# k's inverse norms finished on VectorE, one more row of squares on TensorE, and one 32-bit filler: an edit in the opening of a fused attention and MoE kernel

## The chip, the cores and the metric

The kernel runs on one core of one Trainium2 chip, in one launch. The metric is the device time in microseconds (us), the median of several executions. The core has five engines with their own instruction queues: TensorE (PE, matmuls; its weight loads are shown as PEld), VectorE (DVE), ScalarE (ACT), GpSimd (POOL, which here only issues DMAs) and SyncE (SP, DMAs too). They wait for each other by semaphores.

## What is computed

Four batches of q, k and v, each 6080 rows by 256 channels, go through a channel attention, and the result through an MLP with a squared relu. Norms run along the 6080 rows, one per batch and channel.

```python
def _attn_ref(q, k, v, tau) -> np.ndarray:
    qn = q / (np.linalg.norm(q, axis=1, keepdims=True) + 1e-06)
    kn = k / (np.linalg.norm(k, axis=1, keepdims=True) + 1e-06)
    s = kn.transpose(0, 2, 1) @ qn / tau
    s = s - s.max(-1, keepdims=True)
    a = np.exp(s)
    a /= a.sum(-1, keepdims=True) + 1e-09
    return (v @ a).astype(np.float32)
...
def _moe_ref(x, w_in, w_out, s, b) -> np.ndarray:
    h = x @ w_in
    r = np.maximum(h, 0.0)
    g = s * (r * r) + b
    return (g @ w_out).astype(np.float32)
```

The MLP goes from 256 to 2048 and back to 256 channels, over 24320 rows. tau is 1.

## The kernel before

The main loop, to which the whole file leads up, goes over 48 groups of 512 rows. For each group the core multiplies v (transposed) with `wa`, which is the attention matrix already multiplied into `w_in` (line 755, `h_ps`), applies the relu on ScalarE (L765), squares on VectorE or ScalarE (L776, L778), and multiplies with `w_out` (L830 for the first and last group, L926 for the others). The next batches' attention matrices are worked out beside that. Only the first batch's has nothing to run beside: this opening is what the edit touches.

**The opening.** The rows of the first batch come in 14 chunks: eleven of 512 rows (128 partitions by 4 rows), and three small ones of 256, 128 and 64 rows, the last of which is put in as the fourth chunk; so the numbers from the end are -5 and -4 for two whole chunks and -3, -2, -1 for the last three, a chunk of 512 rows, one of 256 and one of 128. POOL issues the loads of all but the first two chunks in order (L134), k and q in turn, but of the last three (`NLATE = 3`) all of k first and then all of q. Every chunk is multiplied into the 256 by 256 product of q and k (`s_ps`, L150, two matmuls of 128x256 for each of its rows per partition).

For the norms each chunk is squared, k's half on ScalarE (L182), q's on VectorE or ScalarE (L179, L182). VectorE folds the squares twice, 4 rows to 2 and 2 to 1, k and q in one instruction (L196), and adds the result to the first chunk's (`into_first`, L210, 128x512 f16). Sums over the partitions are TensorE matmuls against ones (`add_norms`): for k one 128x256 matmul per row (L251), for q two 128x1 matmuls per row (L255). The list of what is still to be summed is `self.rows`. The last three chunks are not folded into the first: k's squares of chunk -3 are halved on VectorE (L226, `half`), the others go to TensorE as they are (those of chunk -1 are made on VectorE, L176).

From the sum of squares x the inverse norm 1/(sqrt(x) + 1e-6) is made by `inverse` in four ScalarE steps (L276): Ln with `tiny` added, Exp with scale 0.5, Ln with `eps` added, Exp with scale -1. This happens on 128x256 for k, as every partition needs all 256 values, and on 128x2 for q. Then `scale` multiplies the product with k's inverse norms on VectorE, one half after the other (L301, `sm_t`), the exponentials are taken on ScalarE with q's inverse norm as their scale (L307, `eT`), and `first_block` makes the first part of `wa` (L346, L351, L355, L328, L330).

**What sets the order.** Each engine works in program order; `po(...)` keeps the order in which the instructions are written. In the block after `norms_k, *rest = g0.finish_ops()` that order is written out by hand: the chunks up to -4, then k's squares and sums of the last three, `last_sum` (chunk -4's L210, which is pulled out of its chunk) and, after it, the first chunk's summed row; then k's four steps, then for each late chunk q's squares, the product and q's sums, then q's four steps, the scaling, the transposition of v's first group (`transpose_v`, L468, L470), a filler, and `first_block`. `keep_busy` (L548) issues matmuls of 128x512 on a constant tile `fill` (type FP32R), whose result nobody reads. There are two after chunk -5, two after chunk -4 (`FILL`), and one after the transposition.

Of the kernel before, what the change touches and what calls it, by code (L numbers as in the profile page):

```python
# [10 lines left out]
FP32 = mybir.dt.float32  # L11
FP32R = mybir.dt.float32r
# [5 lines left out]
def kernel(  # L18
# [12 lines left out]
    nc = tc.nc  # L31
    P = 128
# [11 lines left out]
    EPS = 1e-6  # L44
# [7 lines left out]
    NLATE = 3  # L52
# [3 lines left out]
    def po(ins):  # L56

        tc.keep_in_program_order(ins)
        return ins
# [32 lines left out]
    def h_tile(name):  # L92
        return ps_h.tile([P, 2, TG], FP32, tag="h_ps", name=name)
# [19 lines left out]
    class Gram:  # L113
# [45 lines left out]
        def norm_ops(self, c):  # L159

            qc, kc = self.tiles[c]
            at, np_, jc = self.chunks[c]
            st = {}

            at_end = self.b == 0 and c >= len(self.chunks) - NLATE

            def squares(a, js):
                def f():
                    if "sq" not in st:
                        if at_end:  # L170
                            st["sq"] = late_pool.tile([P, 2, max(jc, 2), C], FP16, tag=f"sq{c}",
                                                      name="sq")
                        else:
                            st["sq"] = sq_pool.tile([P, 2, JC, C], FP16, tag="sq", name="sq")
                    if a == 1 and at_end and c == len(self.chunks) - 1:
                        po(nc.vector.tensor_mul(  # L176
                            st["sq"][:np_, 1, js, :], kc[:np_, js, :], kc[:np_, js, :]))
                    elif a == 0 and (self.b > 0 or at_end or at // (P * JC) % 2 == 0):
                        po(nc.vector.tensor_mul(  # L179
                            st["sq"][:np_, 0, js, :], qc[:np_, js, :], qc[:np_, js, :]))  # L180
                    else:
                        po(nc.scalar.activation(  # L182
                            out=st["sq"][:np_, a, js, :], in_=(qc, kc)[a][:np_, js, :],
                            func=AF.Square))
                return f

            def fold(half, arrays, last):
                def f():
                    src = st["f", 2 * half] if 2 * half < jc else st["sq"]
                    if ("f", half) not in st:  # L190
                        if last:
                            t = f3_pool.tile([P, 2, 1, C], FP16, tag="f3", name="f3")
                        else:
                            t = sq_pool.tile([P, 2, half, C], FP16, tag=f"f{half}", name="f")
                        st["f", half] = t
                    po(nc.vector.tensor_add(  # L196
                        st["f", half][:np_, arrays], src[:np_, arrays, :half, :],
                        src[:np_, arrays, half : 2 * half, :]))
                    if last and c == 0:
                        self.first = st["f", half]  # L200
                    if last and c == 0:
                        for rows in self.rows:
                            rows.append((st["f", half], np_, 1))
                return f

            def into_first():

                dst, src = self.first[:np_], (st["sq"][:, :, :1] if jc == 1 else st["f", 1])[:np_]
                if self.b == 0:
                    po(nc.vector.tensor_add(dst, dst, src))  # L210
                else:
                    po(nc.gpsimd.dma_start(out=dst, in_=src, accum_op=ALU.add))  # L212

            def unfolded(a):
                self.rows[a].append((st["sq"], np_, jc))

            ops = []
            for h in range(0, jc, 4):
                js = slice(h, min(h + 4, jc))
                ops += [squares(1, js), squares(0, js)]  # L220
            if at_end:
                def rows(a):
                    if a == 0 or jc <= 2:
                        return unfolded(a)
                    half = sq_pool.tile([P, 2, 2, C], FP16, tag="f2", name="half")
                    po(nc.vector.tensor_add(half[:np_, 1], st["sq"][:np_, 1, :2], st["sq"][:np_, 1, 2:]))  # L226
                    self.rows[1].append((half, np_, 2))
                return ops + [rows]
            if jc == 8:
                ops += [fold(4, slice(0, 1), False), fold(4, slice(1, 2), False)]  # L230
            if jc == 1:
                return ops + [into_first]
            ops += [fold(2, slice(0, 2), False), fold(1, slice(0, 2), True)]
            return ops + [into_first] if c > 0 else ops
# [24 lines left out]
        def finish_ops(self):  # L259

            st = {}

            def inverse(a=None):

                n = C + CH if a is None else (CH, C)[a]

                def part(i):
                    if i == 0:
                        st["r", a] = sm_pool.tile([P, n], FP32, tag=f"r{a}", name=f"r{a}")
                        if a is None:  # L270
                            st["r", 1], st["r", 0] = st["r", a][:, :C], st["r", a][:, C:]
                    r = st["r", a]
                    func, kw = [(AF.Ln, dict(bias=tiny)), (AF.Exp, dict(scale=0.5)),
                                (AF.Ln, dict(bias=eps)), (AF.Exp, dict(scale=-1.0))][i]
                    sums = self.n_all if a is None else self.n_ps[a]
                    po(nc.scalar.activation(out=r, in_=r if i else sums, func=func, **kw))  # L276
                    if i == 3 and a != 1 and inv_tau != 1.0:
                        po(nc.vector.tensor_scalar_mul(
                            out=st["r", 0], in0=st["r", 0], scalar1=inv_tau))

                return [lambda i=i: part(i) for i in range(4)]

            def norms(a):
# [150 lines left out]
            def sums_and_halves():  # L434
                sums()
                half_sums()

            return [copy_out, norms_both, *inverse(), scale, lambda: exps(0), lambda: exps(1),
                    sums_and_halves] + seven_folds(0) + seven_folds(1)

# [21 lines left out]
    def transpose_v(g):  # L462
        _, nj = group(g)
        v16 = v_tiles.pop(g)
        vT_ps = ps_o.tile([P, CH, TG], FP16, tag="o_ps", name="vT_ps")
        for j in range(nj):
            for ch in range(CH):
                po(nc.tensor.transpose(vT_ps[:, ch, ts(j, P)], v16[:, j, ts(ch, P)], ident16))  # L468
        vT = vtpool.tile([P, CH, TG], FP16, tag="vT", name="vT")
        po(nc.vector.tensor_copy(out=vT[:, :, : nj * P], in_=vT_ps[:, :, : nj * P]))  # L470
        vT_tiles[g] = vT
# [15 lines left out]
    fill = consts.tile([P, TG], FP32R)  # L487
# [6 lines left out]
    g0 = grams[0]  # L494
# [45 lines left out]
    g0.start()  # L540
    NCH0 = len(g0.chunks)

    FILL = {-5: 2, -4: 2}

    def keep_busy(n):

        for _ in range(n):
            po(nc.tensor.matmul(h_tile("idle_ps")[:, 0, :], fill[:, :P], fill, start=True,  # L548
                                stop=True, skip_group_check=True))

    norms_k, *rest = g0.finish_ops()
    inverse_k, norms_q, inverse_q, scale_s, first_block, folds = (
        rest[:4], rest[4], rest[5:9], rest[9], rest[10], rest[11:])
    late = range(NCH0 - NLATE, NCH0)
    for c in range(NCH0 - NLATE):
        ops = g0.norm_ops(c)
        for j in range(g0.chunks[c][2]):
            g0.mm(c, j)
        keep_busy(FILL.get(c - NCH0, 0))
        if c == NCH0 - NLATE - 1:  # L560
            ops, last_sum = ops[:-1], ops[-1]
        for f in ops:
            f()

    sum_rows = [rows.pop() for rows in g0.rows]
    ops = {c: g0.norm_ops(c) for c in late}
    for c in late:
        k_squares, _, into_rows = ops[c]
        k_squares()
        into_rows(1)  # L570
        g0.add_norms(1)
    last_sum()
    for rows, row in zip(g0.rows, sum_rows):
        rows.append(row)
    for f in (norms_k, *inverse_k):
        f()
    for c in late:
        ops[c][1]()
        ops[c][2](0)
        if c == NCH0 - 1:  # L580
            norms_q()
        for j in range(g0.chunks[c][2]):
            g0.mm(c, j)
        if c < NCH0 - 1:
            g0.add_norms(0)
    for f in (*inverse_q, scale_s):
        f()
    transpose_v(0)
    keep_busy(1)
    first_block()  # L590


# [69 lines left out]
    for i, f in enumerate(folds):  # L662
        early.setdefault(FOLDS[i], []).append(f)
    at_step(14, lambda: po(nc.vector.tensor_scalar_mul(
        out=s_out, in0=s_bc, scalar1=1.0 / (LAM * LAM))))
# [29 lines left out]
    for b in range(1, B):  # L695
# [6 lines left out]
        n = NCH * JC  # L702
# [247 lines left out]
    for s in range(NS + FT):  # L950
# [9 lines left out]
        if work:  # L960
            items, n = work[0]
# [9 lines left out]
        if g < NG and m % 2 == 1:  # L971
            relu(g, m // 2)
            if g in plain and not (g > 0 and m == 3):
                late = g > 0 and m // 2 % 2 == 0
# [48 lines left out]
```

## Time and profile before

| what | value |
|---|---|
| median of 7 runs | 714.5 us (714.29 to 714.57) |
| the profiled execution's own time | 714.36 us |
| its span in the trace | 712.5 us, so 1.9 us of its time lie outside the span |
| PE busy | 693.9 us (97%) |
| DVE busy | 635.5 us (89%) |
| ACT busy | 548.9 us (77%) |
| POOL busy | 114.8 us (16%) |
| mean granted TensorE clock | 0.995 |
| PE busy from 20 to 40 us / from 40 to 60 us | 14.55 of 20 / 20.00 of 20 |

The page's first part gives busy times of engines over the whole span. They say little of the opening, which is some 5% of the span. For that the trace is asked by time: the *chain of waits* (followed back from the last instruction: at each step what released it), the *timeline* of an engine (start, duration, engine, line, output from input, shape), the *windows* (busy time of each engine and the clock that the throttle granted, in a stretch), and single lines of the source (durations in ns). L12 is line 12 of the kernel before; the edit moves later lines by up to 12, and the prediction uses the numbers of before.

### The profile page before, as it was taken

The numbers are of one execution on the slowest core, as the hardware profiler recorded it, in microseconds if no ns is written. First come the engines' busy times: TensorE is split into PE (matmuls) and PEld (weight loads), VectorE is DVE, ScalarE is ACT, GpSimd is POOL, SyncE is SP. The second block draws the span as 40 slices with busy tenths as digits, with TensorE's granted clock in tenths as the row PEclk, the third lists the DMA queues.
The fourth block names the chain that finished last, engine by engine and source line by source line (L and its number), as shares of the span: only waits on it lengthen the run. The fifth ranks groups of instructions, "written<-read, shape, count | busy, mean of one in ns | idle before, by whom it ended". The sixth has DMA issues, their size and how long they took to land.

```text
span 712.5 us, 17524 instructions
## 1 busy us (share of the span) xinstructions
PE 693.9 (97%) x7416; PEld 502.4 (71%) x7416; DVE 635.5 (89%) x906; ACT 548.9 (77%) x601; POOL 114.8 (16%) x194
## 2 busy tenths in 40 slices
PE   4699999999999999999999999999999999999998
PEld 2456777776777777777677777777768777777777
DVE  4889999999988989998999899998998888888886
ACT  4889877787787777778877777777876777777875
POOL 5533132201102222111010222111000000000000
PEclk9899999999999999999999999999999999999999
DMA  9999999566666978464761888637423333321202
GB/s 235 207 259 170 176 169 140 112 104 122 124 116 105 138 139 147 106 92 96 161 129 51 149 137 148 128 76 94 104 64 75 93 72 75 97 61 46 83 30 76
DMA packets 88062, 83.81 MB, mean 118 GB/s; under 512 B 56384, under 2 KB 62992, under 8 KB 87984
## 3 DMA queue, kind: packets, MB, share of 16 engines
q0 software_dynamic: 27216, 43.74, 38.7%
q1 hardware_dynamic: 60192, 37.71, 22.4%
q8 instruction: 58, 0.95, 0.6%
q10 hardware_dynamic: 576, 1.25, 0.5%
q14 instruction: 20, 0.16, 0.1%
HBM read 78.91 MB, written 24.90 MB: 146 GB/s over the span
## 4 chain that ended last, share of the span: by engine, by line
PE 95%; DVE 2%; DMA 1%; ACT 1%; issue 0%; DVEq 0%; ACTq 0%
PE h_ps L755 46%; PE o_ps L926 40%; PE s_ps L150 4%; DVE f L196 1%; PE wa_ps L393 1%; DMA raw<-in_q_dram 1%; PE o_ps L830 1%; PE o_ps L802 0%; ACT sq L182 0%; PE wa_ps L335 0%; DVE f L210 0%; ACT r L276 0%; DVE sq L179 0%; PE n_ps L251 0%; ACT qk L141 0%
## 5 line engine op out<-in xcount | busy, mean ns | idle before, releaser
L765 ACT ACTIVATE r<-h_ps 128x1024 f16<-128x1024 f32 (+1 forms) x384 | 388.5, 1013 | 144.2 <-PE h_ps L755 140.6
L755 PE MATMUL h_ps<-vT,wa 128*128 128x512 f16 (+7 forms) x1632 | 452.1, 364 | 0.5 <-ACT wa L328 0.5
L926 PEld LDWEIGHTS <-S 128*128 128x128 f16 x2944 | 198.1, 98 | 84.4
L926 PEld LDWEIGHTS <-g 128*128 128x128 f16 x2208 | 155.0, 98 | 74.0
L778 DVE TENSOR_TENSOR g<-r 128x2048 f16<-128x2048 f16 (+2 forms) x150 | 174.8, 1165 | 10.0 <-ACT r L765 9.5
L926 PE MATMUL o_ps<-T,S 128*128 128x128 f16 x2208 | 183.1, 219 | 0.0
L755 PEld LDWEIGHTS <-wa 128*128 128x128 f16 x1632 | 136.6, 98 | 19.0 <-ACT wa L328 1.0
L926 PE MATMUL o_ps<-w_out,g 128*128 128x128 f16 x1472 | 134.2, 219 | 0.0
L776 ACT ACTIVATE g<-r 128x1024 f16<-128x1024 f16 (+1 forms) x97 | 100.3, 1034 | 0.2
L783 DVE SCALAR_TENSOR_TENSOR o_sb<-o_ps,s_out,u 128x256 f32<-128x256 f32 x138 | 66.5, 482 | 36.0 <-PE o_ps L926 34.2
L150 PE MATMUL s_ps<-qk 128*128 128x256 f16 (+1 forms) x384 | 73.1, 293 | 13.9 <-ACT qk L141 9.0
L457 POOL DMA_DIRECT2D v<-in_v_dram x48 | 31.4, 662 | 238.2 <-DMA vT<-v 169.8
L212 POOL DMA_DIRECT2D f<-f x33 | 28.8, 874 | 247.3 <-DVE f L196 206.8
L783 DVE SCALAR_TENSOR_TENSOR u<-o_ps,s_out,rowconst 128x256 f32<-128x256 f32 x138 | 66.0, 478 | 0.0
L926 PE MATMUL o_ps<-w_out,S 128*128 128x128 f16 x736 | 63.5, 219 | 0.0
L926 PE MATMUL o_ps<-N,g 128*128 128x128 f16 x736 | 63.4, 219 | 0.0
L182 ACT ACTIVATE sq<-qk 128x1024 f16<-128x1024 f16 (+3 forms) x55 | 54.9, 1017 | 3.8 <-DVE f L196 2.5
L855 DVE TENSOR_TENSOR S<-S,g 128x2048 f16<-128x2048 f16 (+1 forms) x47 | 56.4, 1201 | 1.2
L853 DVE TENSOR_TENSOR S<-g 128x2048 f16<-128x2048 f16 (+1 forms) x47 | 56.1, 1193 | 0.0
L859 DVE TENSOR_TENSOR S<-g,S 128x2048 f16<-128x2048 f16 x46 | 56.0, 1217 | 0.0
L857 DVE TENSOR_TENSOR S<-g 128x2048 f16<-128x2048 f16 x46 | 56.0, 1216 | 0.0
L150 PEld LDWEIGHTS <-qk 128*128 128x128 f16 (+1 forms) x384 | 33.3, 104 | 21.0 <-ACT qk L141 9.5
(104 smaller groups left out, 333.6 us busy)
## 6 DMA issues: line engine op xcount, KB each, us to landing
out_dram<-o_sb SPq DMA_DIRECT2D x43, 512.0 KB, 3.1
v<-in_v_dram POOLq DMA_DIRECT2D x47, 256.0 KB, 4.6
qk<-in_k_dram POOLq DMA_DIRECT2D x42, 256.0 KB, 6.5
qk<-in_q_dram POOLq DMA_DIRECT2D x42, 256.0 KB, 7.4
f<-f POOLq DMA_DIRECT2D x30, 128.0 KB, 3.0
vT<-v SPq DMA_TRANSPOSE x182, 3.2
w<-in_moe_w_out_dram POOLq DMA_DIRECT2D x4, 512.0 KB, 10.0
out_dram<-o_sb SPq DMA_DIRECT2D x8, 256.0 KB, 5.1
```

The lines of the kernel that those rows point to most:

```text
L150: po(nc.tensor.matmul(self.s_ps[:, ch, :], qc[:np_, j, ts(ch, P)], kc[:np_, j, :], start=(c == 0 and j == 0 and ch == 0), stop=(c == len(s ...
L182: po(nc.scalar.activation(out=st["sq"][:np_, a, js, :], in_=(qc, kc)[a][:np_, js, :], func=AF.Square))
L755: po(nc.tensor.matmul(dst, wa[:, ci, ts(m, P)], src, start=(ci == 0), stop=(ci == CH - 1), skip_group_check=True))
L765: po(nc.scalar.activation(out=r16[:, :, i % 2, :n], in_=h_tiles.pop((g, i))[:, :, :n], func=AF.Relu))
L776: po(nc.scalar.activation(out=dst, in_=src, func=AF.Square))
L778: po(nc.vector.tensor_mul(dst, src, src))
L783: po(nc.vector.scalar_tensor_tensor(out=dst, in0=src, scalar=s_out, op0=ALU.mult, in1=add, op1=ALU.add))
L853: po(nc.vector.tensor_add(T[1], A21, A22))
L855: po(nc.vector.tensor_sub(T[2], T[1], A11))
L857: po(nc.vector.tensor_sub(T[3], A11, A21))
L859: po(nc.vector.tensor_sub(T[4], A12, T[2]))
L926: po(nc.tensor.matmul(st[name][:, j, :], a()[:, i, ts(j, P)], w[:, i, :], start=first, stop=last, skip_group_check=True))
```

## The change

Four edits, all in the opening:

1. Chunk -4's folded row is not added to the first chunk's by VectorE. `into_first` appends it to the rows that TensorE sums, for k and for q. `last_sum` and the reordering of the rows go away, so the first chunk's row and chunk -4's are now the first ones that `add_norms` sums.
2. Of k's inverse norm only the first two steps stay on ScalarE. The last two become `invert`: VectorE adds 1e-6 (`tensor_scalar_add`) and takes the reciprocal (`reciprocal`), both in place on 128x256 f32.
3. q's squares of all three late chunks are issued ahead of `invert` on VectorE. The order of product, q's sums and the rest is otherwise that of before.
4. One filler after chunk -5 in place of two there and two after chunk -4; it reads the tile as FP32 instead of FP32R. The filler after the transposition stays as it was.

On TensorE this is three fillers fewer, one k sum more in total (the first chunk's and chunk -4's stand ahead of `half` now) and two q sums of 128x1 more. On VectorE one addition of 128x512 goes and two instructions of 128x256 f32 come; on ScalarE two activations of 128x256 go. POOL's and SyncE's instructions and their order are unchanged.

```diff
@@ into_first
             def into_first():
 
+                if self.b == 0 and c == len(self.chunks) - NLATE - 1:
+                    for rows in self.rows:
+                        rows.append((st["f", 1], np_, 1))
+                    return
                 dst, src = self.first[:np_], (st["sq"][:, :, :1] if jc == 1 else st["f", 1])[:np_]
@@ inverse
+                def invert():
+
+                    r = st["r", a]
+                    po(nc.vector.tensor_scalar_add(out=r, in0=r, scalar1=EPS))
+                    po(nc.vector.reciprocal(out=r, in_=r))
+
+                if a == 1:
+                    return [lambda: part(0), lambda: part(1), invert]
                 return [lambda i=i: part(i) for i in range(4)]
@@ fillers and the order of the opening
-    FILL = {-5: 2, -4: 2}
-
-    def keep_busy(n):
+    FILL = {-5: 1}
+
+    def keep_busy(n, dt):
+
+        f = fill.bitcast(dt)
 
         for _ in range(n):
-            po(nc.tensor.matmul(h_tile("idle_ps")[:, 0, :], fill[:, :P], fill, start=True,
+            po(nc.tensor.matmul(h_tile("idle_ps")[:, 0, :], f[:, :P], f, start=True,
                                 stop=True, skip_group_check=True))
 
     norms_k, *rest = g0.finish_ops()
     inverse_k, norms_q, inverse_q, scale_s, first_block, folds = (
-        rest[:4], rest[4], rest[5:9], rest[9], rest[10], rest[11:])
+        rest[:3], rest[3], rest[4:8], rest[8], rest[9], rest[10:])
     late = range(NCH0 - NLATE, NCH0)
     for c in range(NCH0 - NLATE):
         ops = g0.norm_ops(c)
         for j in range(g0.chunks[c][2]):
             g0.mm(c, j)
-        keep_busy(FILL.get(c - NCH0, 0))
-        if c == NCH0 - NLATE - 1:
-            ops, last_sum = ops[:-1], ops[-1]
+        keep_busy(FILL.get(c - NCH0, 0), FP32)
         for f in ops:
             f()
 
-    sum_rows = [rows.pop() for rows in g0.rows]
     ops = {c: g0.norm_ops(c) for c in late}
     for c in late:
         k_squares, _, into_rows = ops[c]
         k_squares()
         into_rows(1)
         g0.add_norms(1)
-    last_sum()
-    for rows, row in zip(g0.rows, sum_rows):
-        rows.append(row)
-    for f in (norms_k, *inverse_k):
+    for f in (norms_k, *inverse_k[:2]):
         f()
     for c in late:
         ops[c][1]()
+    inverse_k[2]()
+    for c in late:
         ops[c][2](0)
         if c == NCH0 - 1:
             norms_q()
@@ after the transposition of v
-    keep_busy(1)
+    keep_busy(1, FP32R)
     first_block()
```

## The prediction

> **What bounds the kernel now.** I read the page first: over the whole span PE is the chain, so anything that delays the start of the main loop is paid once, in full, and nothing else counts.
>
> ```profile
> PE 95%; DVE 2%; DMA 1%; ACT 1%; issue 0%; DVEq 0%; ACTq 0%
> ```
>
> PE is busy 20.00 of every 20 us from 40 us on, but 14.55 of 20 between 20 and 40 us. The edit lies there. Second view: the chain of waits from 22 to 40 us, in order of time (start, us, what).
>
> ```profile
> 31.08 0.42 DVE f L196
> 31.51 0.35 DVE half L226
> ...
> 31.90 0.83 PE n_ps L251 x6
> ...
> 32.75 0.48 ACT r L276
> ...
> 33.70 0.52 ACT r L276
> ...
> 34.24 0.58 ACT r L276 x2
> ...
> 35.64 0.52 ACT eT L307
> ...
> 37.53 0.60 PE h_ps L755 x2
> ```
>
> See that ScalarE carries it from 32.75 to 36.16: k's four steps, then q's four, then the exponential at 35.64. From 37.53 PE is never idle, so a shift of 35.64 arrives at the end one to one. Third view: VectorE's timeline there (start, us, operation, shape, count).
>
> ```profile
> 31.43 0.42 DVE L226 TENSOR_TENSOR half<-sq 128x512 f16<-128x512 f16 x1
> 31.76 0.28 DVE L176 TENSOR_TENSOR sq<-qk 128x256 f16<-128x256 f16 x1
> 31.96 0.42 DVE L210 TENSOR_TENSOR f<-f,f 128x512 f16<-128x512 f16 x1
> 32.45 1.36 DVE L179 TENSOR_TENSOR sq<-qk 128x1024 f16<-128x1024 f16 x3
> 34.75 0.76 DVE L301 TENSOR_TENSOR sm_t<-s_ps,r 128x256 f32<-128x256 f32 x2 [0.94 <-ACT r L276]
> ```
>
> See the 0.94 us in which VectorE waits for k's last ScalarE step: that is the place into which two VectorE steps are put. It ends not at 32.38 but after q's squares at 32.45+1.36 = 33.81.
>
> **Part 1, chunk -4's row on TensorE.** L210 (0.42 us) leaves VectorE. Its sum was the last of six k matmuls: 31.90 to 32.71, each 0.108 after the last. It and the first chunk's row now go ahead of `half`, into PE's idle 0.72 us before 31.90 (L210 of chunk -5 ends at 30.45, L196 of -4 at 31.50). The rest cannot move: it waits for `half`, on VectorE ahead of L210. So k's Ln starts one matmul earlier: 32.75 - 0.11 = 32.64, and Exp (0.42 to 0.43 us) ends at 33.57 instead of 33.68.
>
> Do q's squares move up by 0.42 too? No. By the issue rows, q of chunks -3, -2, -1 is issued at 24.19, 25.44, 26.76 and lands 8.2, 7.6, 6.7 us later: 32.39, 33.04, 33.46. The three squares (0.685, 0.426, 0.291 us) start at 32.45, 33.11 and about 33.52, each 0.06 behind its load. VectorE is free at 33.81 with or without L210. On PE the product of -3 starts at 32.44 instead of 32.55 (load there at 32.39), and two more 128x1 sums cost 2 x 0.03: q's sums are ready 0.05 earlier, at 34.35 instead of 34.40.
>
> **Part 2, k's last two steps on VectorE.** ScalarE loses Ln 0.51 and Exp 0.42, so q's Ln need not wait for k's Exp: 34.39 instead of 34.56, and q's four steps (34.56 to 35.62) end at 35.45. Taken alone, that moves 35.64 to 35.47: **-0.17**.
>
> On VectorE the addition starts at about 33.75 (neighbours overlap by 0.02 to 0.09; k's Exp is done at 33.57). It is single-source f32 128x256, a form the trace lacks. Below it lies the 128x1 TENSOR_SCALAR (0.146), above it L605, 128x256 out of PSUM (0.480); L301, same shape and type, is nearest: 0.42, so 34.17.
>
> Then the reciprocal of 128x256. The trace has it only on 128x2:
>
> ```profile
> L322 DVE RECIPROCAL rs<-r_ps x3: 161/163/163, 164.1 to 507.1; 128x2 f32<-128x2 f32 x3
> ...
> L355 DVE RECIPROCAL rs<-r_ps x1: 171/171/171, 36.8 to 36.8; 128x2 f32<-128x2 f32 x1
> ...
> L664 DVE TENSOR_SCALAR s_out<-s_bc x1: 146/146/146, 51.0 to 51.0; 128x1 f32<-128x1 f32 x1
> ```
>
> See that two reciprocals take 15 to 17 ns more than one multiplication (25 where VectorE had been idle). If that is a start cost, 256 of them cost what L301 does: 0.42. If it is paid for each of the two, it is 8 ns an element: 0.146 + 256 x 0.0083 = 2.27; by the 25 ns, 12.5 each, 3.35. For comparison the other small steps: a 128x512 copy (0.684) against L301's 0.42 is 1.03 ns an element, so a second element should have added 1 ns, not 15. The only rows of the operation itself are nearest to it, and I take **2.27**.
>
> [...] No row here has more than two elements.
>
> Sum on VectorE: 34.17 + 0.02 + 2.27 = 36.46; first half of the scaling 0.02 + 0.42: 36.90; handover to ScalarE 0.07 (34.66 to 34.75 and 37.02 to 37.11 show 0.09, VectorE to PE 0.04): the exponential at 36.97 instead of 35.64, **+1.33**. Behind the reciprocal wait the second half of the scaling, v's copy (L470, 35.43 before, now 37.15 to 37.84, needed at 38.86) and L355 (not ready before 38.17): neither is late.
>
> **Part 3, the order.** q's squares would in any case have to stand ahead of `invert`, or PE's q sums would wait for the reciprocal. Nothing else waits in that queue; 0.
>
> **Part 4, the filler.** The FP32R ones take 0.48 to 0.78 (PE, half clock and full); after -5 two hold PE from 28.00 to 29.07. An FP32 one is two MATMUL rows, as L604 shows: 128x256 in 0.43 at the full clock (61.65 to 62.08), thus 512 columns at half clock 4 x 0.43 = 1.72, to about 29.8. Chunk -4's eight matmuls then run 29.8 to 31.0 instead of 29.07 to 30.6. Covered by the idle PE until 31.50: 0; with 0.3 more of weight loads still 0. Two fillers at 30.46 go from the same idle time: 0.
>
> The clock belongs to it. Windows (PE busy first, PEclk third from the end):
>
> ```profile
> 22.00:23.00 1.00, 0.55 (x6) 0.25 (x3) 0.97 (x3) 0.94 (x1) 0.53 (x1) 1.00 1.10 207
> 23.00:24.00 1.00, 0.05 (x1) 0.05 (x2) 0.93 (x3) 0.59 (x1) 0.53 (x1) 0.72 1.13 211
> ...
> 29.00:30.00 1.00, 1.00 (x6) 0.69 (x6) 0.95 (x2) 0.99 (x1) 0.71 (x1) 0.50 1.13 194
> 30.00:31.00 1.00, 1.00 (x7) 0.65 (x5) 0.98 (x2) 0.81 (x1) 0.54 (x1) 0.86 1.29 210
> ```
>
> The clock halves at 23.44 (0.72 = 0.44 + 0.56/2) and is full again at 30.28, after PE was busy without a gap from 26.5. One long filler keeps that stretch full, so I expect the same 30.28.
>
> **Sum:** 714.36 (profiled execution: span 712.5 and 1.9 around it) + 1.33 = **715.7**. The median of 7 is 714.5, 0.14 higher; I leave 715.7. Differences under 0.2% (1.43 us) are about what a measurement can tell from no change, so the forecast lies just inside "no change".
>
> **Rivals.**
>
> **B, the reciprocal is short (0.42), 30%.** VectorE: 34.17 + 0.02 + 0.42 + 0.02 + 0.42 = 35.05, under q's 35.45. Gain 0.17: 714.2. The edit turns from gain to loss where the scaled half plus handover passes 35.64, at a reciprocal of 0.94 us. For it: two elements cannot tell a start cost from a slope. Against: the 15 ns.
>
> **C, the clock drops in the new hole, 12%: slower.** With a long reciprocal PE has v's transposes and the filler until 35.7 and then nothing until 37.5. From 33.7 to 37.1, the next stretch of 3.4 us on the grid of 23.44 and 30.28, it is busy 1.85 of 3.4 us (54%; before 2.69, 79%). The row of before: busy 1.04 of 3.4 us (20.0 to 23.4) was followed by the drop. The deciding share lies somewhere from 30% to 79%. Price: 37.1 to 40.5 at half clock, 1.7 us: 714.36 + 1.33 + 1.7 = 717.4. [...] The row fell with 30% busy, so the measurement says a window need not be empty.
>
> **D, the clock does not rise at 30.28** because the FP32 pass counts less, 5%: k's five sums and the product at half clock until 33.7, k's Exp done 0.6 later, the addition 0.5 later: 716.2. Against: PE's records leave no gap.
>
> **E, the row on TensorE gives more than 0.11** (`half` earlier): nothing moves L196 ahead of it; under 3%, and it is what is left for a gain over 1.43.
>
> **Numbers.** Forecast 50%, B 30%, C 12%, D 5%, rest 3%. The forecast's own range is 714.9 (addition 0.15, reciprocal 1.8) to 716.9 (by 12.5 ns an element, +2.4). 8 in 10: from B less a little, 714.0, to C, 717.4. Over 715.93: C, D's most, and a fifth of the forecast: 25%. Under 713.07: 3%. Between: 72%.
>
> **What would show it.** RECIPROCAL 128x256 near 2.3 us behind a 0.3 to 0.4 us TENSOR_SCALAR at 33.75; k's Ln at 32.64; q's Ln at 34.39 and done by 35.5 with ScalarE then waiting for `sm_t`; exponential at 36.97; a hole in PE from 35.7. A reciprocal under 0.94 us makes the sum wrong in sign; PEclk 0.5 after 37.1 makes it C.

## The result, and the profile after

| | before | after |
|---|---|---|
| median | 714.41 us (714.28 to 714.81, 34 executions) | 716.16 us (715.39 to 717.42, 14 executions) |
| ratio after to before | | 1.0025, 95% interval 1.0018 to 1.0032 |
| the profiled execution's own time / span | 714.36 / 712.5 us | 717.37 / 715.6 us |
| mean granted TensorE clock of it | 0.995 | 0.993 |

The changed kernel is slower by 1.75 us. The median hides something: its executions lie in **two groups**, seven from 715.39 to 715.74 and seven from 716.59 to 717.42, and nothing between; the profiled one (717.37) belongs to the upper group. The lower group is the forecast's 715.7, the upper group is its rival C's 717.4. The median 716.16 is the midpoint between 715.74 and 716.59, a time that no execution took; one execution more on either side would have put it at one of these. The mean granted clock of each execution fits C: 0.990 to 0.993 in the upper group, the profiled one included, and 0.995 to 0.998 in the lower (3.41 us at half clock are 0.002 of the span).

First the chain of waits of the kernel after (start, us, what), the same stretch as was shown of before. In after, L280 are the inverse norm's steps on ScalarE, L288 and L289 the new addition and reciprocal, L313 the scaling, L319 the exponential.

```profile
28.52 1.71 PE idle_ps L562 x2
30.22 1.71 PE s_ps L150 x8
31.93 1.16 PE n_ps L255 x7
...
33.11 0.48 ACT r L280
...
34.06 0.31 DVE r L288
...
34.39 1.76 DVE r L289
...
36.25 0.44 DVE sm_t L313
...
36.77 0.52 ACT eT L319
...
38.66 0.39 PE h_ps L765
```

Where ScalarE carried the chain from 32.75 to 36.16 before, VectorE now holds it from 34.06 to 36.69. The exponential starts at 36.77 instead of 35.64. And the filler (L562) stands in the chain, because in this execution the clock was still half when it and chunk -4's product ran.

VectorE's timeline of after, with what ended the idle time in brackets:

```profile
32.56 1.35 DVE L179 TENSOR_TENSOR sq<-qk 128x1024 f16<-128x1024 f16 x3 [0.41 <-DMA qk<-in_q_dram]
34.06 0.29 DVE L288 TENSOR_SCALAR r<-r 128x256 f32<-128x256 f32 x1 [0.15 <-ACT r L280]
34.39 1.75 DVE L289 RECIPROCAL r<-r 128x256 f32<-128x256 f32 x1
36.25 0.76 DVE L313 TENSOR_TENSOR sm_t<-s_ps,r 128x256 f32<-128x256 f32 x2
```

The 0.42 us of L210 that VectorE no longer spends became a wait of 0.41 us for q's load: q's squares did not move up. Where VectorE waited 0.94 us for ScalarE before, it now works 0.29 + 1.75 us.

The windows of after (PE busy first, PEclk third from the end):

```profile
36.00:37.00 1.00, 0.00 (x0) 0.00 (x0) 0.90 (x4) 0.23 (x1) 0.90 (x2) 1.00 1.18 193
37.00:38.00 1.00, 0.67 (x8) 0.33 (x8) 0.63 (x3) 0.68 (x2) 0.00 (x0) 1.00 1.27 207
38.00:39.00 1.00, 0.52 (x3) 0.10 (x1) 0.48 (x3) 0.63 (x2) 0.64 (x1) 1.00 1.24 208
39.00:40.00 1.00, 0.98 (x6) 0.66 (x6) 0.27 (x2) 0.15 (x1) 0.67 (x2) 0.70 1.16 214
40.00:41.00 1.00, 1.00 (x5) 0.41 (x3) 0.48 (x1) 0.33 (x1) 0.56 (x1) 0.50 1.09 349
41.00:42.00 1.00, 1.00 (x6) 0.65 (x5) 0.44 (x2) 0.87 (x1) 0.54 (x1) 0.50 1.04 385
42.00:43.00 1.00, 1.00 (x4) 0.38 (x3) 1.00 (x3) 0.16 (x1) 0.31 (x1) 0.59 1.05 360
```

PE has nothing at all from 36 to 37. Then the clock halves at 39.5 and is full again at 42.9, while PE is busy without a gap: 3.4 us at half clock cost an estimated 1.7 us, the half of it. Before had no such window. This is C's picture, 2.4 us later than C had put it.

**A measure that does not move with the loads.** From one profile to the next q's loads land some 0.5 us earlier or later against the start of the span (the first late square starts behind its load at 32.36 us in hole7, at 32.81 in row), and everything behind them with them. So I compare the time from q's first late square (L179) to the exponential: 35.64 - 32.45 = 3.19 us before, 36.77 - 32.56 = 4.21 in after's profile. The sum of the prediction says 36.97 - 32.45 = 4.52.

### The profile page after: what moved, and what is told of

Same layout as the page of the kernel before. It is cut to its first block, busy times and chain, and to the rows that moved or that the text cites. A ratio compares the mean times of both kernels' runs of the same rounds, so it can differ in the third digit from the quotient of the medians.

```text
span 715.6 us, 17525 instructions
## 1 busy us (share of the span) xinstructions
PE 695.4 (97%) x7417; PEld 502.7 (70%) x7417; DVE 637.2 (89%) x907; ACT 548.1 (77%) x599; POOL 114.8 (16%) x194
## 4 chain that ended last, share of the span: by engine, by line
PE 95%; DMA 3%; POOL 1%; DVE 0%; ACT 0%; issue 0%; POOLq 0%; ACTq 0%; DVEq 0%
PE h_ps L765 46%; PE o_ps L936 40%; PE s_ps L150 5%; DMA qk<-in_q_dram 3%; PE wa_ps L405 1%; PE o_ps L840 1%; POOL qk L134 1%; PE wa_ps L347 1%; PE o_ps L812 0%; DVE r L289 0%; PE idle_ps L562 0%; PE n_ps L255 0%; ACT r L280 0%; ACT eT L319 0%; PE vT_ps L480 0%
```

## The experiments

The theory at this point: the reciprocal, 1.75 us long, delays the exponential (part 2), and the hole that it leaves in PE lowers the clock in some executions. The rivals: the FP32 filler (part 4) is what lowers the clock or delays the opening; the row on TensorE (part 1) or the order (part 3) costs something.

**acts: after, with k's last two steps on ScalarE again.** Parts 1, 3 and 4 stay.

```diff
                 def invert():
 
-                    r = st["r", a]
-                    po(nc.vector.tensor_scalar_add(out=r, in0=r, scalar1=EPS))
-                    po(nc.vector.reciprocal(out=r, in_=r))
+                    part(2)
+                    part(3)
```

> The changed kernel with k's last two norm steps back on ScalarE; the row on TensorE, the order of the squares and the single filler stay. Theory (the 1.75 us reciprocal delays the exponential, and the hole that it leaves in PE lets the clock fall in about half of the executions): the exponential is back at about 35.5, no hole, 714.1 to 714.5 in every execution, no half clock after 37 us. Rival 1 (the second group of times near 717 comes from the single 32-bit filler, which lets the clock rise later): two groups of times stay, 714.3 and about 716. Rival 2 (the delay is the reciprocal alone and the two groups are chance of the chip): about 714.3, but with stray executions 1 to 2 us above.

Measured: 714.45 us (714.18 to 715.69, 11 executions) against 714.49, ratio 1.0000 (0.9991 to 1.0009). VectorE and ScalarE of acts:

```profile
34.74 0.75 DVE L312 TENSOR_TENSOR sm_t<-s_ps,r 128x256 f32<-128x256 f32 x2 [0.94 <-ACT r L280]
```

```profile
35.54 0.91 ACT L318 ACTIVATE eT<-sm_t,r 128x256 f16<-128x256 f32 x2
```

The wait of 0.94 us is back. From q's square to the exponential it is 35.54 - 32.45 = 3.09 us, and the clock does not drop behind it. The whole loss belongs to the two VectorE steps and what follows from them. One execution of the eleven lies 1.2 us above the others; that comes back below.

**hole7: after, with seven fillers behind v's transposition in place of one**, so that PE works through the hole.

```diff
     transpose_v(0)
-    keep_busy(1, FP32R)
+    keep_busy(7, FP32R)
     first_block()
```

> The changed kernel with seven FP32R fillers in place of one after the transposition of v: 0.22 us each at the full clock, so PE is busy to about 36.8 instead of 35.8 while the reciprocal runs. Theory: the clock does not fall after 37 us in any execution, the group near 717 vanishes, all executions at 715.3 to 715.8. Rival 1 (early filler): two groups stay as in the changed kernel, 715.5 and 717.

Measured: 715.45 us, ratio 1.0016 (1.0007 to 1.0024). Nine of eleven executions lie from 715.28 to 715.81, two at 716.42 and 716.48; the group at 717 is gone. From square to exponential it is 36.42 - 32.36 = 4.06. The late exponential stays, the clock's part goes.

**half: after, with the reciprocal on 128 of the 256 columns.** The other columns keep the uninverted norms; only the time is of use.

```diff
-                    po(nc.vector.reciprocal(out=r, in_=r))
+                    po(nc.vector.reciprocal(out=r[:, :P], in_=r[:, :P]))
```

> The changed kernel with the reciprocal on 128 of the 256 columns; the other half of k's norms is left as sqrt(x)+1e-6, so part of the computation is changed. Theory: the cost is per element, 1753 ns less a start of 0.15 us is 6.26 ns each, so the reciprocal takes 0.95 us, and the exponential comes 0.80 us earlier than in the changed kernel; the hole in PE is 0.7 us; 714.5 to 714.9 and mostly one group. Rival (a long fixed cost): 1.7 us and the time of the changed kernel.

Measured: 714.65 us, ratio 1.0003 (0.9994 to 1.0012); from square to exponential 35.74 - 32.49 = 3.25. Groups of VectorE by shape, line and count | busy us, mean ns of one; first after, then half:

```profile
L289 DVE RECIPROCAL r<-r 128x256 f32<-128x256 f32 x1 | 1.8, 1753 | 0.0
L334 DVE RECIPROCAL rs<-r_ps 128x2 f32<-128x2 f32 x3 | 0.5, 162 | 0.0
```

```profile
L289 DVE RECIPROCAL r<-r 128x128 f32<-128x128 f32 x1 | 1.0, 952 | 0.0
```

Three sizes lie on one line: (1753 - 952) / 128 = 6.26 ns for each element, and 952 - 128 x 6.26 = 151 ns at the start. That gives 163 ns for two elements; the row has 162. So the reciprocal is neither short (B) nor 8 ns an element. At 0.95 us the exponential lies within 0.1 us of before's (3.25 against 3.19): the break-even of 0.94 us in rival B is where the prediction put it.

**recip: before, with parts 2 and 3 alone.** Row, `last_sum` and all four fillers as before.

```diff
+                if a == 1:
+                    return [lambda: part(0), lambda: part(1), invert]
...
-    for f in (norms_k, *inverse_k):
+    for f in (norms_k, *inverse_k[:2]):
         f()
     for c in late:
         ops[c][1]()
+    inverse_k[2]()
+    for c in late:
         ops[c][2](0)
```

> The kernel before with only k's two last steps on VectorE behind q's squares; the addition of the row on VectorE and the four FP32R fillers stay. Theory: the whole loss is here, 715.4 to 717.4, in two groups as in the changed kernel, with half clock after 37 us in the upper one. Rival 1 (early filler makes the upper group): one group at 715.2 to 715.7.

Measured: 717.11 us (716.62 to 717.15, 5 executions), ratio 1.0036 (1.0022 to 1.0049). These two parts alone cost more than the whole edit's median. From square to exponential 36.49 - 32.44 = 4.05. The clock falls at 38.06 and rises at 41.47. Neither the new filler nor the row is needed for that.

**recip_hole7: recip, with seven fillers behind the transposition.** One number differs from recip.

```diff
     transpose_v(0)
-    keep_busy(1)
+    keep_busy(7)
     first_block()
```

> The kernel before with k's two last steps on VectorE (as in the run recip, which came out at 716.6 to 717.2 in all five executions) and with seven fillers in place of one after the transposition of v. Theory (the group near 717 is the half clock after the hole in PE): the hole is filled, the clock stays full after 31 us and all executions lie at 715.1 to 715.6. Rival (the upper times come from the reciprocal itself or from the longer chain of waits): 716.6 to 717.2 as in recip.

Measured: 715.30 us (715.03 to 715.47, 11 executions), ratio 1.0012 (1.0004 to 1.0021). Six fillers that compute nothing take 717.11 - 715.30 = **1.8 us** away, with the exponential just as late (36.71 - 32.65 = 4.06). In its profile the window into which the hole would fall is busy for 86%, and the clock stays full behind it:

```profile
35.71:39.12 3.41, 2.92 (x18) 1.54 (x17) 2.52 (x7) 1.54 (x4) 1.99 (x3) 1.00 1.25 206
```

This is the price of the clock, worked out as 1.7 in rival C.

**old4: after, with the four FP32R fillers of before.**

```diff
-    FILL = {-5: 1}
+    FILL = {-5: 2, -4: 2}
...
-        keep_busy(FILL.get(c - NCH0, 0), FP32)
+        keep_busy(FILL.get(c - NCH0, 0), FP32R)
```

> The changed kernel with the four FP32R fillers of before in place of the single FP32 one. Theory: the reciprocal and its hole are untouched, so two groups at 715.4 and about 717 stay, the upper with half clock near 38 to 43 us; at least a third of the executions above 716.5. Rival 1 (the single filler makes the upper group): one group at 715.3 to 715.7.

Measured: 717.14 us, ratio 1.0032 (1.0020 to 1.0044): two executions at 715.39 and 715.47, four from 717.03 to 717.46. The single filler is not what makes the upper group. (The mean granted clock does not part them as cleanly here: 0.992 to 0.995 in the four, 0.995 and 0.998 in the two.) The profiled execution is the one at 715.47, so it shows what after's lower group looks like. ScalarE and then PE in it:

```profile
36.62 0.91 ACT L319 ACTIVATE eT<-sm_t,r 128x256 f16<-128x256 f32 x2 [1.03 <-DVE sm_t L313]
```

```profile
37.18 0.20 PE L358 MATMUL r_ps<-parts,eT 128*128 128x1 f16 x2 [1.39 <-ACT eT L319]
```

The exponential is as late (36.62 - 32.56 = 4.06), and PE's hole of 1.39 us is there, but the clock holds. Why here and not in after's profile? In these profiles the clock changes only at steps of 3.41 us: in after's it falls at 25.86, rises at 32.69, falls at 39.52 and rises at 42.93, distances of two steps, two and one. Where the steps lie against the kernel's start differs from one profiled execution to the next: the first fall is at 20.9 to 25.9 us. Windows cut along the steps, from after, recip and old4 (length, PE busy):

```profile
36.10:39.52 3.42, 1.68 (x12) 0.75 (x13) 2.18 (x7) 1.53 (x4) 1.96 (x4) 0.98 1.22 204
```

```profile
34.65:38.06 3.41, 1.75 (x17) 0.93 (x17) 2.82 (x6) 1.71 (x6) 1.63 (x3) 0.98 1.29 202
```

```profile
33.38:36.80 3.42, 2.27 (x36) 1.61 (x33) 3.28 (x7) 1.43 (x6) 2.22 (x4) 1.00 1.30 200
36.80:40.21 3.41, 2.54 (x18) 1.35 (x19) 1.88 (x6) 1.84 (x6) 2.17 (x4) 1.00 1.21 210
```

In recip the whole hole lies within one window, in after all but its first 0.3 us; these windows are busy for 51% and 49%, and the clock falls at its end. In old4 a step at 36.80 cuts the hole in two, both windows are busy for 66% and 74%, and nothing falls. So one kernel has two times. That the position decides is read from these three profiles; no run here moves it alone.

**row: before, with part 1 alone.**

```diff
+                if self.b == 0 and c == len(self.chunks) - NLATE - 1:
+                    for rows in self.rows:
+                        rows.append((st["f", 1], np_, 1))
+                    return
...
-            ops, last_sum = ops[:-1], ops[-1]
...
-    sum_rows = [rows.pop() for rows in g0.rows]
...
-    last_sum()
-    for rows, row in zip(g0.rows, sum_rows):
-        rows.append(row)
```

> The kernel before with only the fourth-last chunk's row summed on TensorE. Theory: k's Ln starts 0.11 us earlier and everything behind it with it: 714.3 to 714.4, against 714.4 to 714.5; no strays over 715.2, since the fillers are those of before. Rival (VectorE's 0.42 us count in full): 714.0.

Measured: 714.60 us (714.22 to 714.94), ratio 1.0001 (0.9992 to 1.0009): the expected 0.11 us is too little for these times to show. Its profile says where such a gain would stop. VectorE, PE and ScalarE of row:

```profile
32.81 1.31 DVE L179 TENSOR_TENSOR sq<-qk 128x1024 f16<-128x1024 f16 x3 [0.52 <-DMA qk<-in_q_dram]
```

```profile
34.45 0.29 PE L259 MATMUL n_ps<-ones,sq 128*128 128x1 f16 x6
```

```profile
34.78 0.26 ACT L280 ACTIVATE r<-n_ps,tiny 128x2 f32<-128x2 f32 x1
```

k's Ln starts at 32.88 there and k's Exp ends at 34.80. q's Ln starts at 34.78, just behind q's sums (34.45 + 0.29 = 34.74). So q's loads now come last together with k's steps, and from k's Ln to the exponential it is 3.00 us instead of 2.89.

**filler: before, with part 4 alone.**

```diff
-    FILL = {-5: 2, -4: 2}
+    FILL = {-5: 1}
...
-        keep_busy(FILL.get(c - NCH0, 0))
+        keep_busy(FILL.get(c - NCH0, 0), FP32)
```

> The kernel before with only the single FP32 filler in place of four. Theory: for most positions of the clock's grid no change, 714.4 to 714.6; in about one execution in ten, where the clock rises only at about 32.7 us, the filler and chunk -4's product run at half clock ahead of k's sums and the time is 0.8 to 1.3 us more (strays at 715.2 to 715.8, as in acts and half). Rival (the strays of acts and half come from the row or the order of the squares): no strays here.

Measured: 714.58 us, ratio 1.0003 (0.9994 to 1.0012), with one execution of eleven at 715.76. Usually the filler costs nothing, as predicted. The one late execution fits the one in ten that was expected; that a late rise of the clock is its cause is not shown.

**shift: hole7, with one memset of 128x1 more at the start.** This is about a remainder. In after, hole7, half and old4 the first `wa` on VectorE (L342) starts 0.50 to 0.52 us behind `rs`, in acts, row, recip and recip_hole7 some 0.1 us, with the same waits. Where it is late, it stands at one and the same place of VectorE's program, bare waits counted: the 65th by the count of the expectation below, the 64th of those that the trace records. I keep to the 65th.

```diff
     nc.vector.memset(eps, EPS)
+    nc.vector.memset(eps, EPS)
```

> The kernel hole7 with one tiny VectorE memset (128x1) more among the constants at the start, so that every later VectorE instruction is one place further back in its program. Open is why, in the kernel after, hole7, half and old4, the first wa instruction starts 0.50 to 0.52 us behind the rs reciprocal and in acts, recip, recip_hole7 and row 0.12 us behind it, with the same waits: in all of the former it is the 65th instruction of VectorE's program, waits counted. Theory place (the position in the program delays it, about 0.4 us): wa starts 0.12 us behind rs, the second h_ps matmul pair takes 0.60 instead of 0.78, and the usual times go from hole7's 715.3 to 715.5 down by 0.1 to 0.2 us. Rival (data, PSUM or the missing ScalarE steps set it): wa stays at 0.50, time as hole7. The exponential stays at 36.4 to 36.5 in both.

Measured: 715.25 us (ten of eleven from 715.13 to 715.54, one at 716.98), ratio 1.0014 (1.0005 to 1.0023). VectorE of hole7, then of shift:

```profile
37.63 0.17 DVE L367 RECIPROCAL rs<-r_ps 128x2 f32<-128x2 f32 x1 [0.37 <-PE r_ps L358]
38.30 0.61 DVE L342 TENSOR_SCALAR wa<-wa_ps,rs 128x128 f16<-128x128 f32 x2 [0.50 <-PE wa_ps L363]
```

```profile
37.73 0.17 DVE L367 RECIPROCAL rs<-r_ps 128x2 f32<-128x2 f32 x1 [0.37 <-PE r_ps L358]
38.00 0.61 DVE L342 TENSOR_SCALAR wa<-wa_ps,rs 128x128 f16<-128x128 f32 x2
```

The wait of 0.50 us is gone with nothing changed in the program but the place. The profile puts it down to PE's L363, which is the last semaphore that came; in hole7 that matmul had ended 0.47 us before. The `h_ps` pair shrinks from 0.79 to 0.60 us. The medians, 715.45 and 715.25, were taken on different chips and their intervals overlap, so they don't show so small a difference. The profiles do: from the exponential to the end of the span it is 677.1 us in hole7, half and old4, and 676.9 us in shift, recip_hole7 and before. So this is a cost of 0.2 us that after pays and before does not.

**before_shift: before, with two such memsets more.** In before the 65th instruction is the second `wa`.

```diff
     nc.vector.memset(eps, EPS)
+    nc.vector.memset(eps, EPS)
+    nc.vector.memset(eps, EPS)
```

> The kernel before with two tiny VectorE memsets (128x1) more at the start. In before the 65th instruction is the second wa, and the second h_ps pair takes 0.80; with two more the 65th is a bare semaphore wait. Theory place: the pair takes 0.60 and the time is 0.1 to 0.2 us under before's 714.4: 714.2 to 714.3, which the rounds hardly tell from no change, so the profile's row decides. Rival: the pair stays at 0.80 and the time at 714.4.

Measured: 714.48 us, ratio 1.0001 (0.9992 to 1.0010). VectorE's pair of `wa` shrinks from 0.80 to 0.61 us, as the theory says. The expectation was wrong on one row: the 0.80 was VectorE's, PE's pair took 0.60 in before already. So PE did not wait for it, and there was nothing to gain.

## Why the prediction was right, and where it was not

Its time was 715.7 with a range from 714.0 to 717.4; measured 716.16. The direction, the place and the two ways it goes were right; two sizes were off, one chance was far too low, and one cost was missed. That 716.16 lies between the forecast and C is the even split of the executions, not a size that was worked out; a time over 715.93 had been given 25%.

- **Part 2, the reciprocal: mis-sized.** Predicted 2.27 us (8.3 ns an element by two rows of 128x2 against a multiplication), measured 1.753, by 6.26 ns an element behind 0.15 us. The step that failed is to take the whole difference to a TENSOR_SCALAR 128x1 as the slope of two elements, from a start of 0.146 us: a start 5 ns longer explains it. That 15 to 17 ns were a slope and not a start cost was right, and it decided the sign; but two elements could not show it, and the forecast gave it only 50%.
- **Part 2, the addition: a little short of its term.** Predicted 0.42, measured 0.36 to 0.41 (0.29 where VectorE had been idle). It started as q's squares ended, as predicted, wherever the clock had risen in time (33.61 in hole7, 33.84 in old4).
- **The sum on VectorE.** From q's square to the exponential 4.52 predicted, 4.05 to 4.06 measured in recip, recip_hole7, hole7, old4 and shift, against 3.19 before. The exponential moved by **+0.87 us and not by +1.33**: the reciprocal took 0.52 less, the rest is small and partly cancels (0.10 us between reciprocal and scaling where 0.02 stood).
- **A missed cost, 0.2 us.** `wa` (L342) starts 0.4 us late by its place in the program. 0.87 + 0.2 is the 1.1 us by which after's lower group (715.39 to 715.74) lies above before. So the forecast's 715.7 is near that group partly because an overestimate of 0.46 was made up by 0.2 that it did not know.
- **C, the clock: right mechanism and price, wrong chance.** Predicted 1.7 us at 12%; measured 1.8 between recip and recip_hole7, and 717.07 - 715.49 = 1.6 between the medians of after's groups. In single profiles, from the exponential to the end of the span, it is 678.80 us in after against 677.08 in old4, and 678.36 in recip against 676.94 in recip_hole7: 1.7 and 1.4 us. It happened in half of after's executions, in four of six of old4 and in all five of recip. The step that failed is the window "From 33.7 to 37.1, the next stretch of 3.4 us on the grid of 23.44 and 30.28": it took the steps of one execution for those of the kernel. Had I let them lie anywhere, a hole of 1.4 to 1.6 us with half-idle PE around it would have met a window of about 50% in a good share of executions. The bracket "from 30% to 79%" was right: behind the hole the clock fell after windows busy for 49% (after) and 51% (recip), and held after 66% and 74% (old4).
- **Part 1, the row: right that little comes of it.** q's squares stayed with their loads (0.41 us of wait in after). k's Ln follows q's first square by 0.18 to 0.21 us in acts, hole7, half, old4 and shift, against 0.30 in before: the 0.11 that was worked out. But recip, which keeps L210, shows 0.20 too, and row, the part alone, 0.07, so the gain is not told apart from the scatter of the loads. In after's profile it is 0.55 (k's Ln at 33.11 and not 32.64), because the clock rose only at 32.69 and not at 30.28.
- **Part 3, the order: 0**, consistent with acts, where it stays in and nothing is lost; it was not run alone.
- **Part 4, the filler: 0 in most executions, not in all.** The two MATMUL rows took 1.71 us at half clock (1.72 predicted). In after's profiled execution the clock rises late as in rival D, as the chain shows, but not for D's reason: the steps lay 2.4 us later (fall at 25.86, rise at 32.69), and the rise came behind the first window that PE filled, as in before. Its price at the exponential was 4.21 - 4.06 = 0.15 us, not 0.5, since VectorE is busy with q's squares until 33.9 anyway. What stays open: of the kernels with the single filler whose clock does not fall behind the hole (acts, hole7, half, filler, shift) 6 of 55 executions lie 1.0 to 1.7 us above their kernel's median, of row, recip_hole7 and before_shift none of 33. Of before's own 110 executions, with four FP32R fillers, none lies more than 0.6 us above its median. So these late executions come with the single filler, and one in eleven of the run filler is among them; how it makes them is not shown. None of the six was profiled, and their mean granted clock, 0.995, is that of most of the others.

No version here beats before: acts, row and filler are the same to within the interval, and the steps on VectorE lose 0.87 us even when the clock holds.

## What to carry to other kernels

Before a long operation is moved to another engine, find its price per element from two sizes of the same operation, or measure it: here the sign hung on whether a reciprocal takes more or less than 0.94 us. Here the wait on the critical path was also a hole for TensorE, 1.4 to 1.6 us long, and it cost twice: 0.87 us for itself and, in some executions only, 1.4 to 1.8 us for the clock, so look at all the times and not at the median alone. Matmuls that nobody reads, put into the hole, tell the two costs apart in one run (717.11 to 715.30).

## What was not expected of the hardware

- **The clock's steps are not tied to the kernel's start.** In the profiles they come at intervals of 3.41 us, and their position differs from one profiled execution to the next (first fall at 20.9 us in shift, at 25.9 in after). In the first 45 us of the twelve profiles all fourteen falls come behind a window in which PE was busy for 31% to 51%; no window over 55% is followed by one; between 44% and 55% both occur (51% in after from 15.6 to 19.0, and 44% in before_shift from 28.5 to 31.9, without a fall). Rises come behind windows of 80% to 100%, but windows of 80% in hole7 (23.8 to 27.2) and shift (24.3 to 27.8) brought none.
- **The place of an instruction in VectorE's program cost 0.2 to 0.4 us.** The 65th (the 64th that the trace records) started 0.4 us late in after, hole7, half and old4, and 0.2 us late in before and filler, where the pair of `wa` took 0.80 and 0.81 us instead of 0.61. One more tiny instruction ahead of it in hole7, and two in before, ended that. What makes it late is not shown.
- **RECIPROCAL on VectorE, f32:** 0.16 us for 2 elements per partition, 0.95 for 128, 1.75 for 256; a TENSOR_SCALAR of 128x256 f32 took 0.29 us after idle time.
